# Attention scores by head instead of by pair of heads: products of 64 rows and 72 columns in place of 128 rows and 144 columns, in an attention and mixture-of-experts kernel on one Trainium2 core

## The chip, the cores and the metric

The kernel runs on one core of a Trainium2 chip. The metric is the time of one execution on the device, in microseconds (us). Matrix products run on TensorE (PE in the profile; its loads of the stationary operand are listed apart, as PEld). VectorE is DVE, ScalarE is ACT, GpSimd is POOL, and SP is the engine that issues most of the DMAs.

## The reference

```python
B, H, S, D = 8, 8, 576, 64          # attention
Sp = S // 8                          # 72: keys and values are averaged over 8 rows
k_p = k.reshape(B, H, Sp, 8, D).mean(axis=3)
v_p = v.reshape(B, H, Sp, 8, D).mean(axis=3)
scores = matmul(q, k_p^T) / sqrt(D)  # per head: 576 x 72, over 64 elements
attn = softmax(scores)
x = (attn @ v_p) as 4608 tokens x 512
# mixture of experts: the token's best of 4 groups, then the best of that group's 4 experts
h = relu(x[mask] @ w1[g, e]); ye = h @ w2[g, e]      # 512 -> 1024 -> 512
out[mask] = gate * ye
```

All data is float32.

## The kernel before

The work goes batch by batch (8 batches of 576 tokens). For each batch the attention part pools keys and values, computes scores and their softmax and multiplies by the pooled values; then the batch's most frequent expert is applied to all its tokens (`up`, line 532, and `down`, lines 553 and 563). Tokens of other experts are taken by a loop at the end of the program.

A batch's 576 query rows are five chunks: four of 128 rows and one of 64 (`CH`). For each chunk, `sc` computes the scores of all eight heads. The heads stand in four pairs g. The transposed queries `qT` have a pair's two heads one above the other: 64 partitions of the first head, 64 of the second. The transposed pooled keys `kT` are 128 partitions by 144 columns a pair, with the first head's 72 columns filled in the upper 64 partitions, the second head's 72 columns in the lower 64, and zeros in the two other quarters. So one product a pair, over all 128 partitions, gives both heads' scores side by side. The chunk's query rows are the stationary operand (`lhsT`), `kT` is streamed past it (`rhs`). Each float32 product of this kind appears in the profile as two loads and two MATMULs, so that a chunk's four products are eight of each.

The scores stand in one PSUM tile of two banks (`ss`, two pairs to a bank). From there VectorE takes the maxima (`mx`, line 298) and subtracts them (`sb`, line 304), ScalarE takes the exponential (line 305), VectorE sums (`su_`), GpSimd or VectorE divides (`nm`), and TensorE transposes the probabilities (`px_`, line 331; `pm`, line 343) for the product with the values (`av`, line 358).

The order of the work is written by hand in four lists: START and FIRST for the beginning and batch 0, STEADY for batches 1 to 6, LAST for batch 7. While a batch's expert runs, the next batch's attention is done between its pieces: `m.up:0:0`, then `n.sc:1 n.mx:1 n.sb:1`, then `m.up:0:1`, and so on. TensorE, SP and VectorE follow these lists in program order; ScalarE and GpSimd follow them in START, and GpSimd's and ScalarE's order in the rest is set by the framework's scheduler. `warm` (line 824) are products of a matrix of ones, which fill TensorE's waits at the start.

Of the kernel before, what the change touches and what calls it, by code (L numbers as in the profile page):

```python
# [8 lines left out]
F32 = mybir.dt.float32  # L9
# [4 lines left out]
ALU = mybir.AluOpType  # L14
# [4 lines left out]
SP = 72  # L19
NG = H // 2  # L20
# [65 lines left out]
def attn_moe(ctx: ExitStack, tc: tile.TileContext, q, k, v, wg, we, w1, w2, out):  # L86
    nc = tc.nc
    tt, ts, stt = nc.vector.tensor_tensor, nc.vector.tensor_scalar, nc.vector.scalar_tensor_tensor
# [53 lines left out]
    sm = ctx.enter_context(tc.tile_pool(name="sm", bufs=2))  # L142
# [16 lines left out]
    class Att:  # L159
# [127 lines left out]
        def sc(s, c):  # L287
            n = CH[c][1]
            ps = s.ss[c] = ps_s.tile([128, 2, 512], F32, name="sc")
            for g in range(NG):  # L290
                nc.tensor.matmul(ps[0:n, g // 2, 144 * (g % 2):144 * (g % 2) + 144], lhsT=s.qT[c][:, g, 0:n], rhs=s.kT[:, g, :],  # L291
                                 start=(g % 2 == 0), stop=(g % 2 == 1))

        def mx(s, c):
            n = CH[c][1]
            scv = s.ss[c][0:n, :, 0:288].rearrange("p u (x s) -> p u x s", s=SP)
            mx = s.m[c] = sm.tile([128, 2, 4], F32, name="mx")
            red(out=mx[0:n], in_=scv, axis=AX.X, op=ALU.max)  # L298

        def sb(s, c):  # L300
            n = CH[c][1]
            scv, mx = s.ss[c][0:n, :, 0:288].rearrange("p u (x s) -> p u x s", s=SP), s.m[c]
            p = s.p[c] = sm.tile([128, 2, 4, SP], F32, name="p")
            tt(out=p[0:n], in0=scv, in1=mx[0:n].unsqueeze(3).broadcast_to([n, 2, 4, SP]), op=ALU.subtract)  # L304
            nc.scalar.activation(out=p[0:n], in_=p[0:n], func=AF.Exp)  # L305

        def su_(s, c):
# [568 lines left out]
```

## Time and profile before

| | |
|---|---|
| median of 3 runs | 615.87 us (615.83 to 618.83) |
| the profiled execution | 614.83 us |
| its span, first to last instruction | 612.7 us |
| TensorE (PE) busy | 589.0 us, 96% of the span |
| loads of its stationary operand (PEld) busy | 525.6 us, 86% |
| VectorE, ScalarE, GpSimd busy | 404.8, 281.8, 253.8 us |
| MATMULs of `sc` (line 291) | 320, of 3841 |
| mean granted TensorE clock | 0.988 of full speed |

The profile is of one execution. Around its span lie 2.1 us of the execution's time. Matmuls overlap in time, each starting before the one ahead has ended, so that a group's pace (start to start) is shorter than the duration of one; pieces of the chain of waits, which count each moment once, are read as paces. In a shape such as 128\*64 128x144 the first pair is the stationary operand's partitions and columns, the second the streamed operand's.

### The profile page before, as it was taken

To read this page: it belongs to the slowest core of one execution; us is meant where nothing else is said; L and a number is where in the kernel's file an instruction comes from. 1 tells how busy PE (TensorE), PEld (TensorE's weight loads), DVE (VectorE), ACT (ScalarE), POOL (GpSimd) and SP (SyncE) were. 2 spreads that over 40 slices of the span, in tenths; PEclk is the share of its full clock that TensorE was granted. 3 is DMA by queue.
4 is the path that set the end of the run, shared out by engine and by line. 5 is a ranking of instruction groups with operands and counts; after the bars stand their busy time and mean duration, and the time that the engine had idled before them with its cause. 6 is when DMAs were issued, how large, how long until landed. Compare 5 with 4: busy or idle time off the path is not lost.

```text
span 612.7 us, 10857 instructions
## 1 busy us (share of the span) xinstructions
PE 589.0 (96%) x3841; PEld 525.6 (86%) x3841; DVE 404.8 (66%) x1000; ACT 281.8 (46%) x585; POOL 253.8 (41%) x255
## 2 busy tenths in 40 slices
PE   6969999999999999999999999999999999999996
PEld 5858887789988999789988998789978998899874
DVE  4886998879774696548774696549673783347231
ACT  3544635366444653555344653455434643243121
POOL 3034546056423663275424663275424662253100
PEclk8998999999999999999999999999999999999999
DMA  6476415255517542454517552484517200541911
GB/s 186 101 243 113 157 36 113 77 200 200 112 52 242 171 83 75 138 186 124 110 49 242 173 88 68 148 347 115 112 39 245 92 1 2 177 176 26 381 68 40
DMA packets 118761, 81.30 MB, mean 133 GB/s; under 512 B 76327, under 2 KB 95271, under 8 KB 118321
## 3 DMA queue, kind: packets, MB, share of 16 engines
q1 hardware_dynamic: 112656, 70.83, 39.4%
q10 hardware_dynamic: 6016, 9.70, 4.4%
q8 instruction: 32, 0.52, 0.4%
q14 instruction: 25, 0.20, 0.1%
q0 software_dynamic: 32, 0.04, 0.0%
HBM read 75.01 MB, written 28.38 MB: 169 GB/s over the span
## 4 chain that ended last, share of the span: by engine, by line
PE 78%; DVE 13%; DMA 3%; ACT 2%; issue 2%; SPq 1%; POOL 0%; DVEq 0%; POOLq 0%
PE mm L532 28%; PE mm L553 26%; PE sc L291 5%; PE tp L358 5%; PE mm L563 5%; DVE kp L208 3%; PE tp L343 2%; DMA kv<-in_v_dram 2%; DMA sw<-in_moe_w_dram 1%; DVE ht L539 1%; PE tp L331 1%; ACT kb L226 1%; PE tp L371 1%; DVE px L320 1%; DVE xt L363 1%
## 5 line engine op out<-in xcount | busy, mean ns | idle before, releaser
L532 PE MATMUL mm<-xt,w 128*128 128x256 f32 (+1 forms) x1536 | 224.5, 301 | 3.8 <-DVE ht L539 1.6
L532 PEld LDWEIGHTS mm<-xt,w 128*128 128x128 f32 x1536 | 208.7, 190 | 7.1 <-issue 1.7
L553 PE MATMUL mm<-w,ht 128*128 128x512 f32 x768 | 187.7, 396 | 0.0
L518 POOL TENSOR_TENSOR w<-sw,w 128x1024 fp32r<-128x1024 f32 x54 | 131.7, 2456 | 95.2 <-ACT w L517 90.9
L553 PEld LDWEIGHTS mm<-w,ht 128*128 128x128 f32 x768 | 140.8, 188 | 29.3 <-issue 0.8
L534 ACT ACTIVATE ht<-mm 128x256 fp32r<-128x256 f32 (+1 forms) x128 | 52.2, 408 | 112.2 <-PE mm L532 110.8
L539 DVE SCALAR_TENSOR_TENSOR ht<-mm,ht 128x256 fp32r<-128x256 f32 (+1 forms) x192 | 60.5, 344 | 35.0 <-ACT ht L534 34.9
L517 ACT CAST w<-sw 128x1024 fp32r<-128x1024 f32 x64 | 65.5, 1048 | 23.2 <-DMA sw<-in_moe_w_dram 13.4
L320 POOL TENSOR_TENSOR px<-p,su 128x96 f32<-128x96 f32 (+1 forms) x72 | 24.5, 360 | 96.3 <-DVE su L312 53.2
L298 DVE TENSOR_REDUCE mx<-sc 128x8 f32<-128x576 f32 (+1 forms) x40 | 29.9, 748 | 36.5 <-PE sc L291 36.5
L291 PE MATMUL sc<-kT,qT 128*128 128x144 f32 (+1 forms) x320 | 47.4, 292 | 0.0
L291 PEld LDWEIGHTS sc<-kT,qT 128*128 128x128 f32 (+1 forms) x320 | 42.6, 184 | 2.3 <-issue 1.6
L324 POOL TENSOR_TENSOR p<-p,su 128x576 f32<-128x576 f32 (+1 forms) x36 | 41.4, 1149 | 2.8
L558 ACT ACTIVATE y<-mm,gm 128x512 f32<-128x512 f32 x32 | 21.9, 684 | 36.8 <-PE mm L553 36.7
L305 ACT ACTIVATE p<-p 128x576 f32<-128x576 f32 (+1 forms) x40 | 27.3, 683 | 21.8 <-DVE p L304 21.7
L310 DVE TENSOR_REDUCE su<-p 128x8 f32<-128x576 f32 (+1 forms) x40 | 29.9, 746 | 8.9 <-ACT p L305 7.9
L569 DVE TENSOR_TENSOR y<-mm,y 64x512 f32<-64x512 f32 x8 | 5.5, 682 | 44.7 <-ACT y L568 44.7
L363 DVE TENSOR_TENSOR xt<-tp,xt 128x320 fp32r<-128x320 f32 (+2 forms) x68 | 29.3, 437 | 7.9 <-ACT xt L359 6.2
L359 ACT CAST xt<-tp 128x320 fp32r<-128x320 f32 (+2 forms) x68 | 26.1, 384 | 17.1 <-PE tp L358 15.1
L208 DVE TENSOR_REDUCE kp<-kv 128x128 f32<-128x1024 f32 x16 | 31.0, 1971 | 2.7 <-DMA kv<-in_k_dram 2.7
L304 DVE TENSOR_TENSOR p<-sc,mx 128x576 f32<-128x576 f32 (+1 forms) x40 | 30.2, 754 | 3.3
L230 POOL TENSOR_TENSOR kv<-kv 128x512 f32<-128x512 f32 x13 | 16.8, 1292 | 32.8 <-DMA kv<-in_v_dram 32.3
(206 smaller groups left out, 739.0 us busy)
## 6 DMA issues: line engine op xcount, KB each, us to landing
sw<-in_moe_w_dram SPq DMA_DIRECT2D x72, 512.0 KB
xscr<-xt SPq DMA_DIRECT2D x8, 2304.0 KB
kv<-in_k_dram SPq DMA_DIRECT2D x16, 512.0 KB
kv<-in_v_dram SPq DMA_DIRECT2D x16, 512.0 KB
out_dram<-y ACTq DMA_DIRECT2D x32, 256.0 KB
q<-in_q_dram SPq DMA_DIRECT2D x112, 72.0 KB
kv<-in_moe_w_dram SPq DMA_DIRECT2D x6, 512.0 KB
ph<-xscr SPq DMA_DIRECT2D x2, 1152.0 KB
```

What stands on the lines that cost most here:

```text
L208: red(out=s.kp[:, 2 * u:2 * u + 2, :], in_=s.k[u].rearrange("p g (j d) -> p g d j", j=8), axis=AX.X, op=ALU.add)
L291: nc.tensor.matmul(ps[0:n, g // 2, 144 * (g % 2):144 * (g % 2) + 144], lhsT=s.qT[c][:, g, 0:n], rhs=s.kT[:, g, :], start=(g % 2 == 0), sto ...
L324: eng.tensor_tensor(out=p[0:n], in0=p[0:n], in1=su[0:n].unsqueeze(3).broadcast_to([n, 2, 4, SP]), op=ALU.mult)
L358: nc.tensor.matmul(ps[:, 0:n], lhsT=flat(l[:, g]), rhs=r, start=(i == 0), stop=(i == len(ops) - 1))
L363: tt(out=s.xt[:, 1, g, sl], in0=s.ta[g][:, 0:n], in1=s.xt[:, 0, g, sl].bitcast(F32), op=ALU.subtract)
L517: nc.scalar.copy(out=wh, in_=raw)
L518: (nc.vector if eng == "v" else nc.gpsimd).tensor_tensor(out=wl, in0=raw, in1=wh.bitcast(F32), op=ALU.subtract)
L532: nc.tensor.matmul(ps[:, 0:n], lhsT=l[:, kc, fs], rhs=xt[:, r, kc, sl], start=(kc == 0 and i == 0), stop=(kc == 3 and i == 2))
L534: nc.scalar.activation(out=ht[:, sl], in_=ps[:, 0:n], func=AF.Relu)
L539: stt(out=ht[:, at:at + hi - lo], in0=ps[:, lo - o:hi - o], scalar=0.0, in1=ht[:, lo:hi].bitcast(F32), op0=ALU.max, op1=ALU.subtract)
L553: nc.tensor.matmul(ps, lhsT=s.ht[f][:, 640 * l + o:640 * l + o + 128], rhs=s.w[2, f // 2][r][:, f % 2, :], start=(i == 0), stop=(i == 23))
L563: nc.tensor.matmul(ps, lhsT=s.ht[f][:, 512:640], rhs=s.w[2, f // 2][r][:, f % 2, :], start=(i == 0), stop=(i == 15))
```

## The change

`sc` computes each head by itself. For a pair g and a head x of it, the product takes the 64 partitions of that head in `qT` and `kT` and the 72 columns that are filled, so that the quarters of zeros are no longer streamed. A chunk has eight products in place of four, each of half the partitions and half the columns. The heads x = 0 go to the first bank of the PSUM tile and the heads x = 1 to the second. `mx` and `sb` read the tile by another access pattern (pair, then bank, then the 72 columns), and `sb` writes the probabilities in the order in which they stood before. The number of elements is the same in each.

```diff
         def sc(s, c):
             n = CH[c][1]
             ps = s.ss[c] = ps_s.tile([128, 2, 512], F32, name="sc")
             for g in range(NG):
-                nc.tensor.matmul(ps[0:n, g // 2, 144 * (g % 2):144 * (g % 2) + 144], lhsT=s.qT[c][:, g, 0:n], rhs=s.kT[:, g, :],
-                                 start=(g % 2 == 0), stop=(g % 2 == 1))
+                for x in range(2):
+                    r = slice(64 * x, 64 * x + 64)
+                    nc.tensor.matmul(ps[0:n, x, SP * g:SP * g + SP], lhsT=s.qT[c][r, g, 0:n], rhs=s.kT[r, g, SP * x:SP * x + SP],
+                                     start=(g == 0), stop=(g == NG - 1))
 
         def mx(s, c):
             n = CH[c][1]
-            scv = s.ss[c][0:n, :, 0:288].rearrange("p u (x s) -> p u x s", s=SP)
-            mx = s.m[c] = sm.tile([128, 2, 4], F32, name="mx")
+            scv = s.ss[c][0:n, :, 0:288].rearrange("p x (g s) -> p g x s", s=SP)
+            mx = s.m[c] = sm.tile([128, NG, 2], F32, name="mx")
             red(out=mx[0:n], in_=scv, axis=AX.X, op=ALU.max)
 
         def sb(s, c):
             n = CH[c][1]
-            scv, mx = s.ss[c][0:n, :, 0:288].rearrange("p u (x s) -> p u x s", s=SP), s.m[c]
+            scv, mx = s.ss[c][0:n, :, 0:288].rearrange("p x (g s) -> p g x s", s=SP), s.m[c]
             p = s.p[c] = sm.tile([128, 2, 4, SP], F32, name="p")
-            tt(out=p[0:n], in0=scv, in1=mx[0:n].unsqueeze(3).broadcast_to([n, 2, 4, SP]), op=ALU.subtract)
+            pv = p[0:n].rearrange("p u (y x) s -> p (u y) x s", x=2)
+            tt(out=pv, in0=scv, in1=mx[0:n].unsqueeze(3).broadcast_to([n, NG, 2, SP]), op=ALU.subtract)
             nc.scalar.activation(out=p[0:n], in_=p[0:n], func=AF.Exp)
```

On TensorE, in a batch's steady part, the chunks' scores (`sc`) stand between `up` products (`mm<-xt,w`). Before (the program counts a float32 product once here, and prints the output's size):

```order
L532 MATMUL mm<-xt,w 128x256 x12
L291 MATMUL sc<-kT,qT 128x144 x4
L532 MATMUL mm<-xt,w 128x320 x12
L532 MATMUL mm<-xt,w 128x256 x12
L331 MATMUL tp<-ident,px 96x128 x2
L343 MATMUL tp<-ident,p 128x128 x4
L532 MATMUL mm<-xt,w 128x320 x12
L291 MATMUL sc<-kT,qT 64x144 x4
```

The same places on TensorE now, where every line number from `sc` on has grown by three or four:

```order
L536 MATMUL mm<-xt,w 128x256 x12
L294 MATMUL sc<-kT,qT 128x72 x8
L536 MATMUL mm<-xt,w 128x320 x12
L536 MATMUL mm<-xt,w 128x256 x12
L335 MATMUL tp<-ident,px 96x128 x2
L347 MATMUL tp<-ident,p 128x128 x4
L536 MATMUL mm<-xt,w 128x320 x12
L294 MATMUL sc<-kT,qT 64x72 x8
```

Nothing else moved on TensorE: four products became eight at each of the 40 places (32 chunks of 128 rows, 8 of 64), and all around them stands as it stood. SP's order is the same too, and VectorE's but for buffer numbers.

On ScalarE the scheduler moved a few instructions by one place. Near the start of a steady batch, before (`ht<-mm` is the `up` piece's relu, `p<-p` the exponential of a chunk's scores, `y<-y,gm` the last rows of the batch before):

```order
L570 ACTIVATE y<-y,gm 64x512
L571 DMA out_dram<-y 64x512
L534 ACTIVATE ht<-mm 128x320
L305 ACTIVATE p<-p 128x576
L534 ACTIVATE ht<-mm 128x256
L332 CAST pr<-tp 96x2x128
```

And now, at the same place on ScalarE:

```order
L574 ACTIVATE y<-y,gm 64x512
L575 DMA out_dram<-y 64x512
L309 ACTIVATE p<-p 128x576
L538 ACTIVATE ht<-mm 128x320
L538 ACTIVATE ht<-mm 128x256
L336 CAST pr<-tp 96x2x128
```

The exponential now stands ahead of one relu that it followed. This recurs once in each steady batch; in FIRST and in the first steady batch there are three more such exchanges on ScalarE, and one on GpSimd.

## Rows read from the trace of the kernel before

**Rows 1.** The page: busy time by engine, TensorE's granted clock in 40 slices.

```profile
PE 589.0 (96%) x3841; PEld 525.6 (86%) x3841; DVE 404.8 (66%) x1000; ACT 281.8 (46%) x585; POOL 253.8 (41%) x255
...
PEclk8998999999999999999999999999999999999999
```

**Rows 2.** Windows by stage: length, busy time of each engine (instructions), clock, DMA.

```profile
0.00:62.00 62.00, 49.55 (x352) 44.21 (x353) 43.38 (x82) 28.32 (x63) 19.02 (x42) 0.89 0.60 159
62.00:125.50 63.50, 60.23 (x380) 52.21 (x379) 56.08 (x141) 29.99 (x72) 24.65 (x30) 1.00 0.38 107
...
194.08:262.66 68.58, 68.51 (x437) 61.68 (x437) 46.21 (x111) 33.88 (x70) 32.00 (x31) 1.00 0.45 133
```

**Rows 3.** The chain of waits, in order of time, in one steady batch.

```profile
208.64 1.75 PE mm L532 x12
210.39 0.98 PE sc L291 x8
211.37 3.18 PE mm L532 x24
...
221.47 1.76 PE mm L532 x12
223.23 1.12 PE sc L291 x8
224.35 3.38 PE mm L532 x24
```

**Rows 4.** The chain of waits in START and FIRST, batch 0.

```profile
22.69 0.98 PE sc L291 x8
...
30.08 8.05 DMA sw<-in_moe_w_dram
...
50.98 1.58 PE sc L291 x8
```

**Rows 5.** Timeline around a chunk of 128 rows, TensorE and its loads.

```profile
134.95 1.05 PEld L291 LDWEIGHTS sc<-kT,qT 128*128 128x128 f32 x8
135.07 1.15 PE L291 MATMUL sc<-kT,qT 128*128 128x144 f32 x8
```

**Rows 6.** Timeline around a chunk of 64 rows, in brackets the idle time before.

```profile
154.59 0.93 PEld L291 LDWEIGHTS sc<-kT,qT 128*64 128x64 f32 x8 [0.19 <-issue]
154.59 1.19 PE L291 MATMUL sc<-kT,qT 128*64 128x144 f32 x8
155.72 0.19 PEld L532 LDWEIGHTS mm<-xt,w 128*128 128x128 f32 x1 [0.20 <-issue]
```

**Rows 7.** Timeline: loads behind which little is streamed, 128 and 64 partitions.

```profile
23.39 0.98 PEld L454 LDWEIGHTS tp<-wr,ht 128*128 128x128 f32 x8
...
575.25 0.29 PEld L701 LDWEIGHTS tp<-kT,q 64*128 64x128 f32 x2
```

**Rows 8.** Groups of loads by form: busy us, mean ns of one.

```profile
L291 PEld LDWEIGHTS sc<-kT,qT 128*128 128x128 f32 x256 | 34.8, 194 | 0.7 <-issue 0.2
L291 PEld LDWEIGHTS sc<-kT,qT 128*64 128x64 f32 x64 | 7.8, 143 | 1.6 <-issue 1.4 <-PE tp L343 0.2
L701 PEld LDWEIGHTS tp<-kT,q 64*128 64x128 f32 x2 | 0.3, 184 | 0.0
L448 PEld LDWEIGHTS tp<-ht,rp 32*64 32x64 f32 x8 | 0.7, 130 | 0.7 <-issue 0.7
```

**Rows 9.** Timeline in START: one part of the array, then two column halves by turns.

```profile
19.22 0.19 PEld L448 LDWEIGHTS tp<-ht,rp 32*64 32x64 f32 x2 [0.17 <-issue]
19.57 0.20 PEld L446 LDWEIGHTS tp<-ht,vp 128*64 128x64 f32 x4 [0.17 <-issue]
...
19.22 0.43 PE L448 MATMUL tp<-ht,rp 32*64 32x128 f32 x2
19.58 0.44 PE L446 MATMUL tp<-ht,vp 128*64 128x128 f32 x4
```

**Rows 10.** Timeline: transposes of a 64-row chunk, 64 partitions, between full-height products.

```profile
162.94 0.17 PEld L331 LDWEIGHTS tp<-ident,px 64*96 64x96 f32 x2 [0.19 <-issue]
163.05 0.33 PEld L343 LDWEIGHTS tp<-ident,p 64*128 64x128 f32 x4
...
163.10 0.41 PE L343 MATMUL tp<-ident,p 64*128 64x64 f32 x4
```

**Rows 11.** The page: groups of VectorE that read the scores.

```profile
L298 DVE TENSOR_REDUCE mx<-sc 128x8 f32<-128x576 f32 (+1 forms) x40 | 29.9, 748 | 36.5 <-PE sc L291 36.5
...
L304 DVE TENSOR_TENSOR p<-sc,mx 128x576 f32<-128x576 f32 (+1 forms) x40 | 30.2, 754 | 3.3
```

**Rows 12.** Timeline of ScalarE in a steady batch, around a chunk's exponential.

```profile
206.58 0.44 ACT L534 ACTIVATE ht<-mm 128x320 fp32r<-128x320 f32 x1 [1.60 <-PE mm L532]
206.91 0.68 ACT L305 ACTIVATE p<-p 128x576 f32<-128x576 f32 x1
208.02 0.38 ACT L534 ACTIVATE ht<-mm 128x256 fp32r<-128x256 f32 x1 [0.43 <-PE mm L532]
```

## The prediction

> **What bounds the kernel now.** I read the page first. TensorE is busy for 96% of the span, and its granted clock is at full speed (the level of 2.4 GHz) in all but the first few slices [rows 1]. Busy shares are averages, so the windows by stage come next: in a steady batch TensorE is busy for 68.51 of 68.58 us, while the next busiest engine, VectorE, has 46.21 [rows 2]. What TensorE takes longer or shorter there goes into the time whole. Only the first two stages have idle time on it: 12.5 us in the first 62 us, 3.3 us in the next 63.5 [rows 2]. The chain of waits confirms the place: in a steady batch it runs along TensorE from piece to piece, and each chunk's scores stand in it with 0.98 us at 128 rows and 1.12 us at 64 [rows 3]. Of batch 0's five chunks only the second and the last stand in the chain; behind the second comes a weight transfer of 8.05 us [rows 4].
>
> So I count 7 batches with four chunks of 128 rows on the path, and one of batch 0's: 29 of 32. Of the 64-row chunks all 8 count.
>
> **What a chunk's scores cost now.** Eight MATMULs of 144 columns in 0.98 us are 0.122 us each. The eight loads run beside them and start with the same steps (1.05 us against 1.15 for the eight) [rows 5]: streaming sets the pace, loads are hidden.
>
> How fast could loads alone go? Where only 20 columns are streamed behind a load, eight loads take 0.98 us; one lasts 0.19, so the step is (0.98 - 0.19)/7 = 0.112 us for 128 columns of stationary operand. With 64 partitions and the same 128 columns, two loads take 0.29, one 0.184: a step of 0.29 - 0.184 = 0.11 us [rows 7, 8]. Half the partitions save nothing. Columns do: 64 of them last 0.143 us and 32 partitions with 64 columns 0.130, against 0.194 for 128 columns [rows 8], and two of 0.130 end within 0.19 [rows 9], a step of 0.06.
>
> **The change, part by part.** *Streaming.* 72 columns should take half of 144: 0.061 us a MATMUL.
>
> *Loads.* The products double and their loads do not shrink at 128 rows: 16 loads of 128 columns in place of 8. The two heads of a pair use different halves of the array. If the halves work side by side, each has 8 loads one after another, at 0.112 us a step, and the streaming (0.061) hides under them. If one waits for the other, a step for both is 0.224. No row shows two halves that lie one above the other. The nearest shows two halves side by side: four loads and four MATMULs in two column halves take 0.20 and 0.44 us, where two loads and two MATMULs in a single part take 0.19 and 0.43 [rows 9]. I take 0.112, with 0.061 and 0.224 as the bounds.
>
> The Trainium skill, TensorEngine Tiling (Array Packing), Key Properties, says that tiles are independent and can load and multiply in parallel. By that rule the step is 0.112; the trace agrees for column halves, and no run here shows row halves yet.
>
> *Passing to a smaller part of the array and back.* This is the part of which the diff says nothing. Wherever the trace goes from full-size products to a smaller part, the load waits 0.17 to 0.20 us and is not fetched ahead: at the 64-row chunk going in and coming out [rows 6], at 64-partition transposes [rows 10], in START [rows 9]. A chunk of 128 rows shows no such gap now [rows 5]. Its price comes from the chain: a 64-row chunk with the `up` products around it takes 1.76 + 1.12 + 3.38 = 6.26 us, a 128-row chunk with the same number around it 1.75 + 0.98 + 3.18 = 5.91 [rows 3]. The eight MATMULs are equally wide, so passing in and out costs 0.35 us. In it lies the first load, bare, of 64 columns; at 128 columns that is 0.112 - 0.06 = 0.05 more. So 0.40 us for each 128-row chunk, newly paid, since its products are now of half height; the 64-row chunks pay their 0.35 already.
>
> *A chunk of 128 rows* then takes 0.40 + 7 steps of 0.112 + 0.061 for the last streaming = 1.245 us against 0.98: 0.265 more. 29 of them: +7.7 us.
>
> *A chunk of 64 rows* has loads of 64 columns, 0.06 a step, that just hide under 0.061 of streaming: 8 x 0.061 = 0.49 against 0.98, and the same passing: 0.49 less. 8 of them: -3.9 us.
>
> *VectorE.* The maxima and the subtraction read the same 576 elements in runs of 72, in another order: 748 and 754 ns [rows 11]. I take no change. If each took half as long again, that is 0.75 us a chunk, 3.8 us a batch, on an engine with 22 us to spare there [rows 2]; what it would hide behind is the next `up` products on TensorE, 3.18 us after each chunk [rows 3].
>
> *ScalarE.* The exponential that now stands ahead of a relu takes 0.68 us [rows 12]. That relu is late by 0.5 to 0.7 us, and what waits behind it, the `upd` subtraction, frees one of three PSUM tiles of `up`. TensorE comes back to that tile two `up` pieces later, some 3 us (24 products take 3.18 [rows 3]). I put it at nothing; without that cover it would be 0.6 us a batch, 4 us in all.
>
> **The sum.** 7.7 - 3.9 = +3.8 us. All 32 chunks on the path would make +4.6, batch 1's hidden in the idle time of its stage +3.2. The error of the passing price (0.05 a chunk) is 1.5 us either way, that of the load step (0.106 to 0.12) -1.2 to +1.6. The profiled execution took 614.83 us (span 612.7 and 2.1 around it), so it becomes 618.6. The median of the runs, 615.87, lies 1.0 above the profiled execution, and I forecast the median: 619.6 us, with its own range of 616.5 to 623. A change under 0.5% (3.1 us) is what a measurement of this kernel can hardly tell from none, and the forecast lies just outside.
>
> **The rivals.** *The halves take turns at loading.* A step for both halves is then 0.224 us: 0.40 + 7 x 0.224 + 0.061 = 2.03, or 1.05 more a chunk, +30.4 us for 29. The 64-row chunks would gain only 0.98 - 8 x 0.12 = 0.02. About 645 us. For it speaks only that no row shows row halves; against it, the column halves [rows 9].
>
> *A load waits for its own half's MATMUL to end.* A step is 0.112 + 0.061 = 0.173 and a 128-row chunk takes 0.69 more: +20 us, with little gained at 64 rows, about 636 us. Against it: full-height loads run beside MATMULs of the same rows today [rows 5], and the four 64-partition loads from 163.05 to 163.38 run over the four transposes from 163.10 to 163.51 [rows 10].
>
> The Trainium skill, TensorE: Matmul & The Clock Gate, The mechanism, has that rule: a load overlaps with MATMULs in flight only if their row groups differ. By it this rival would hold; rows 5 and 10 show overlap on the same rows, so I give it little.
>
> *Faster.* This would need one thing: that in half-height products loads cost no more than the streaming. At a step of 0.061 a 128-row chunk takes 0.40 + 0.43 + 0.06 = 0.89, and all gain: 29 x -0.09 - 3.9 = -6.5, about 609 us. The two kinds of chunk balance at a step of 0.093 (29 x (7 x 0.093 - 0.519) = 3.8). The 0.11 of the 64-partition load [rows 7] speaks against it, though it is a single pair.
>
> The Trainium skill, TensorEngine Tiling, Theoretical Speedup, promises up to twice the speed for a dimension of 64 or less. Taken as half the time of each chunk it would give more than this rival; rows 7 have loads that do not halve.
>
> *Nothing to measure.* A step of 0.10, or a passing price nearer 0.35, leaves +1 to +2 us: 617 to 618.
>
> **Chances.** The forecast (side-by-side halves, loads set the pace) 0.72; turns 0.12; loads that wait 0.03; faster 0.05; nothing to measure 0.08. Within the forecast I give 0.20 to the part under 3.1 us. So slower 0.52 + 0.15 = 0.67, same 0.20 + 0.08 = 0.28, faster 0.05. The range takes in the forecast and "nothing to measure" and leaves out the rest, 0.20: 615 to 624.
>
> **What the profile after would show.** 128-row chunks: 16 MATMULs of 64\*128 by 72 in pairs that start together, pairs 0.11 us apart; in the chain 0.8 to 0.9 us for the scores themselves, 0.2 us of waiting for nothing named at each load that goes in or out, and `up` products behind them at 3.38 in place of 3.18. 64-row chunks: pairs 0.06 apart. A steady batch: 68.58 + 4 x 0.265 - 0.49 = 69.15 us, with VectorE and ScalarE as busy as now. I am wrong if pairs don't start together (a batch then takes some 4 us more), if they come faster than 0.09, or if the gaps on going in and out are missing: then 29 x 0.40 = 11.6 us fall away, and the time is some 608.

## The result and the profile after

| | before | after |
|---|---|---|
| median of 20 runs each | 615.85 us (614.39 to 620.35) | 624.55 us (618.62 to 626.76) |
| ratio of the times | | 1.0106, interval 1.0081 to 1.0131 |
| the profiled execution | 614.83 us | 624.49 us |
| its span | 612.7 us | 622.3 us |
| its mean granted clock | 0.988 | 0.976 |

The change makes the kernel slower. The times of after stand on two levels: 13 of the 20 took 624.0 to 626.8 us at a mean granted clock of 0.972 to 0.979, the other seven 618.6 to 621.9 at 0.982 to 0.992. Before has two levels as well, 13 runs at 614.4 to 616.4 us and seven at 618.4 to 620.4. These 20 have no clock on record; of 40 more runs of before, timed beside the experiments, six took 618.6 to 619.4 us, at 0.982 to 0.987, and none of the 40 had a clock under 0.982. The ratio lies below that of the medians (1.014), because the middle time of before falls on its lower level and that of after on its upper. A ratio goes by the runs within 1.5% of the fastest of their kernel, which leaves out one run here, 624.45 us of sc0_half.

Applied to 615.85 the ratio gives 622.4 us, inside the range of 615 to 624; the median of 624.55 lies 0.55 above it. The lowest times differ by 618.62 - 614.39 = 4.2 us, close to the forecast of +3.8. What the forecast did not have is the upper level of after, with its lower clock.

The page after: TensorE's busy time and clock, the groups of `sc`, and those of VectorE that read the scores (lines 291, 298 and 304 before, now 294, 301 and 308).

```profile
PE 599.2 (96%) x4161; PEld 527.6 (85%) x4161; DVE 402.6 (65%) x1000; ACT 281.1 (45%) x585; POOL 253.2 (41%) x255
...
PEclk8597999999999999999999999999999999999999
...
L308 DVE TENSOR_TENSOR p<-sc,mx 128x576 f32<-128x576 f32 (+1 forms) x40 | 30.2, 754 | 3.3
...
L301 DVE TENSOR_REDUCE mx<-sc 128x8 f32<-128x576 f32 (+1 forms) x40 | 29.9, 748 | 36.3 <-PE sc L294 35.9
```

Against [rows 1] TensorE is busy for 10.2 us more, and the second of the clock's 40 digits is 5 where it was 9. VectorE's two groups are where they were, 748 and 754 ns [rows 11].

The chain of waits of after in the steady batch of [rows 3], and the start of the next batch:

```profile
200.63 1.05 PE sc L294 x16
201.68 3.85 PE mm L557 x16
...
215.68 1.75 PE mm L536 x12
217.43 1.04 PE sc L294 x16
218.48 3.38 PE mm L536 x24
...
229.03 1.76 PE mm L536 x12
230.79 0.65 PE sc L294 x16
231.43 3.38 PE mm L536 x24
...
269.71 1.05 PE sc L294 x16
```

A chunk of 128 rows with the `up` products around it now takes 1.75 + 1.04 + 3.38 = 6.17 us, where [rows 3] have 5.91: 0.26 more. A chunk of 64 rows takes 1.76 + 0.65 + 3.38 = 5.79 in place of 6.26: 0.47 less. From one batch's first scores to the next one's, 200.63 to 269.71, are 69.08 us; before, the same two marks lie 68.58 apart [rows 2].

Timeline of after around the 128-row chunk, TensorE:

```profile
217.36 1.11 PE L294 MATMUL sc<-kT,qT 64*128 64x72 f32 x16
```

The same of its loads:

```profile
217.36 0.97 PEld L294 LDWEIGHTS sc<-kT,qT 64*128 64x128 f32 x16 [0.19 <-issue]
```

Sixteen loads end within 0.97 us: the eight of a half would need 7 x 0.112 + 0.19 = 0.97 by themselves, so the other half's eight lie beside them. Ahead of the first load stands the idle 0.19 us that [rows 6] show around a 64-row chunk and [rows 5] don't show.

The windows by stage of after, against [rows 2]:

```profile
0.00:62.00 62.00, 52.46 (x368) 45.70 (x369) 39.77 (x76) 26.00 (x57) 14.56 (x38) 0.78 0.55 146
...
194.08:262.66 68.58, 68.51 (x474) 60.88 (x474) 45.54 (x110) 33.29 (x70) 32.22 (x30) 1.00 0.45 130
```

The steady stage has the same idle time on TensorE as before (0.07 us) and full speed. The first stage had a clock of 0.89 and has 0.78. So the 9.6 us between the two spans come from two places. Where batch 2's first scores begin (125.35 us before, 131.45 after), 6.1 us are already lost. The six batches whose scores follow make 3.0 at +0.50 each; 0.5 I did not place.

The start, in windows of TensorE before (busy time, granted clock, DMA share and GB/s). These rows are not among those of the prediction:

```profile
16.00:18.00 2.00, 2.00 (x12) 0.57 0.42 20
18.00:20.00 2.00, 1.70 (x16) 1.00 0.91 190
20.00:32.00 12.00, 11.91 (x104) 1.00 0.46 129
```

And after:

```profile
14.00:16.00 2.00, 2.00 (x11) 0.50 0.26 52
16.00:18.00 2.00, 2.00 (x17) 0.50 0.40 22
18.00:20.00 2.00, 2.00 (x14) 0.50 0.89 181
20.00:32.00 12.00, 12.00 (x64) 0.50 0.17 40
32.00:34.00 2.00, 2.00 (x18) 0.88 0.36 89
```

A granted clock of 0.50 is the level of 1.2 GHz, 1.00 that of 2.4. Before, TensorE comes to full speed between 16 and 18 us, while it works on batch 0's first scores; after, only between 32 and 34. In the 12 us from 20 to 32 it is busy throughout in both, and gets through 104 MATMULs before and 64 after.

What stands on TensorE where the clock did not rise, timeline of after:

```profile
16.45 1.99 PE L294 MATMUL sc<-kT,qT 64*128 64x72 f32 x16
18.37 1.11 PE L278 MATMUL tp<-ident,q 128*128 128x128 f32 x4
```

The same transposes in the timeline of before:

```profile
17.95 0.60 PE L278 MATMUL tp<-ident,q 128*128 128x128 f32 x4
```

Before, these four ran at full speed, in 0.60 us where there are now 1.11. The chain of waits of after, at batch 0's first two chunks, at the routing behind them (`wr`, line 458), at the weights that it chooses and at batch 0's last chunk:

```profile
16.52 1.92 PE sc L294 x16
...
26.02 1.92 PE sc L294 x16
27.94 1.84 PE tp L458 x8
...
35.37 8.20 DMA sw<-in_moe_w_dram
...
56.37 0.70 PE sc L294 x16
```

The second chunk's scores begin at 26.02 in place of 22.69 us [rows 4], 3.3 later, and take 1.92 in place of 0.98. The routing's products are then 4.3 late and take 1.84 us, where the chain of before has 0.81 (from 23.68 us). Together that is the +5.3 with which the transfer starts, at 35.37 in place of 30.08 us; the last chunk's scores follow at 56.37 in place of 50.98 [rows 4], +5.4. The first chunk now stands in the chain too; before, VectorE's work behind a transfer of values stood there.

### The profile page after: what moved, and what is told of

Read it like the earlier page. It is cut to its first block, busy times and chain, and to the rows that moved or that the text cites. A ratio compares the mean times of both kernels' runs of the same rounds, so it can differ in the third digit from the quotient of the medians.

```text
span 622.3 us, 11497 instructions
## 1 busy us (share of the span) xinstructions
PE 599.2 (96%) x4161; PEld 527.6 (85%) x4161; DVE 402.6 (65%) x1000; ACT 281.1 (45%) x585; POOL 253.2 (41%) x255
## 4 chain that ended last, share of the span: by engine, by line
PE 77%; DVE 13%; DMA 3%; ACT 2%; SPq 2%; issue 2%; POOL 1%; DVEq 0%; POOLq 0%
PE mm L536 28%; PE mm L557 25%; PE sc L294 5%; PE tp L362 5%; PE mm L567 5%; DVE kp L208 3%; PE tp L347 2%; DMA q<-in_q_dram 1%; DMA sw<-in_moe_w_dram 1%; DVE ht L543 1%; PE tp L335 1%; ACT kb L226 1%; PE tp L375 1%; DVE px L324 1%; DVE xt L367 1%
## 5 line engine op out<-in xcount | busy, mean ns | idle before, releaser
L294 PEld LDWEIGHTS sc<-kT,qT 64*128 64x128 f32 (+1 forms) x640 | 37.3, 183 | 7.8 <-issue 4.2
L294 PE MATMUL sc<-kT,qT 64*128 64x72 f32 (+1 forms) x640 | 43.2, 276 | 0.0
```

Of the source, the lines that this page charges most:

```text
L294: nc.tensor.matmul(ps[0:n, x, SP * g:SP * g + SP], lhsT=s.qT[c][r, g, 0:n], rhs=s.kT[r, g, SP * x:SP * x + SP], start=(g == 0), stop=(g == ...
```

## The experiments

The first four kernels behind after let some chunks go head by head and the rest by pair; pass_only is the kernel before with one product added, and the last three change one thing in the products of all chunks. The steady theory is that of the prediction (16 loads side by side, passing in and out), the clock theory that the half-height products of the start cost some 5 us more through TensorE's clock.

| kernel | head by head are | median us | ratio to before, interval |
|---|---|---|---|
| after | all 40 chunks | 624.55 | 1.0106 (1.0081 to 1.0131) |
| start_full | all but batch 0's four of 128 rows | 621.78 | 1.0084 (1.0052 to 1.0116) |
| start_half | batch 0's first three | 620.1 | 1.0064 (1.0038 to 1.009) |
| sc0_half | batch 0's first | 615.3 | 1.0016 (0.9983 to 1.0049) |
| c4_only | the eight of 64 rows | 612.91 | 0.9954 (0.9933 to 0.9976) |
| pass_only | none; one small product behind each of 28 chunks | 626.14 | 1.016 (1.0119 to 1.0201) |
| same_half | all, on one half, without the second heads | 654.04 | one run |
| full72 | all, over 128 partitions | 641.19 | one run |
| x_outer | all, first one half's four products | 642.31 | one run |

The kernel before, timed beside them, stood at medians of 615.24 us (for start_full, start_half, c4_only, same_half) and 615.32 (for the others).

**start_full: the start by pair, the rest head by head.**

```diff
+        def half(s, c):
+            return s.b > 0 or c == 4
...
         def sc(s, c):
             n = CH[c][1]
             ps = s.ss[c] = ps_s.tile([128, 2, 512], F32, name="sc")
+            if not s.half(c):
+                for g in range(NG):
+                    nc.tensor.matmul(ps[0:n, g // 2, 144 * (g % 2):144 * (g % 2) + 144], lhsT=s.qT[c][:, g, 0:n], rhs=s.kT[:, g, :],
+                                     start=(g % 2 == 0), stop=(g % 2 == 1))
+                return
...
```

What is left out lets `mx` and `sb` read either layout.

> Batch 0's first four chunks by pair of heads, as before; all other chunks by head. Theory A (two causes: in the steady batches the passing in and out and the loads, 7 x 0.5 = 3.5 us; at the start the half-height products, under which TensorE's clock stays at half longer): the start is as before, clock 0.89 in the first 62 us, whole run 3 to 4 us above before, 619 to 619.5. Theory B (the longer half clock at the start is chance, not the products' height): it stays as often as with the whole change, median 622 to 624.5.

Measured: 618.91 to 622.87 us in six runs. The start is nearly as before again, in the windows of this kernel; the clock is up between 18 and 20 us:

```profile
16.00:18.00 2.00, 2.00 (x11) 0.50 0.39 21
18.00:20.00 2.00, 2.00 (x17) 0.89 0.88 176
20.00:32.00 12.00, 11.93 (x104) 1.00 0.46 130
```

No run had a mean clock under 0.980, where 13 of 20 had it with the change. Two of the six stand at 0.980, a little under the lowest of before (0.982), and no trace shows their start. So the long stretch at 1.2 GHz hangs on batch 0's 128-row chunks, at least for the most part. But the median is some 2.5 us above what was expected. The profiled execution (622.67) shows 2.1 us of it, in a place of its own: in the first steady batch TensorE waits 2.06 us for VectorE. VectorE there:

```profile
135.53 2.63 DVE L339 TENSOR_TENSOR px<-p,su 128x96 f32<-128x96 f32 x2
138.19 2.84 DVE L343 TENSOR_TENSOR p<-p,su 128x576 f32<-128x576 f32 x1
```

GpSimd in the same stretch:

```profile
132.82 2.40 POOL L537 TENSOR_TENSOR w<-sw,w 128x1024 fp32r<-128x1024 f32 x1 [3.85 <-ACT w L536]
135.66 4.76 POOL L537 TENSOR_TENSOR w<-sw,w 128x1024 fp32r<-128x1024 f32 x2 [0.43 <-ACT w L536]
```

Beside the two products of GpSimd (135.66 to 140.42) VectorE's two lines last 2.63 us (two operations) and 2.84. In the profile before they last 0.43 and 0.76 and start between two such products, at 132.80 and 133.26 us; GpSimd's end at 132.50 and start again at 133.50. ScalarE's cast ahead of GpSimd waits 1.78 us for a weight transfer here. The Trainium skill, GPSIMD Engine Reference, Specifications, says that GpSimd shares its way to SBUF with VectorE and that instructions with two SBUF inputs contend; these two have two, and the rows agree. How often this meeting happens, and whether the change has a part in it, these runs don't settle: c4_only's profiled execution has it too, and some runs of before lie on a level that would fit it (3 of the 23 beside this kernel at 618.8 to 619.4 us, seven of the first 20 at 618.4 to 620.4), though no trace was kept of one.

**start_half: only the start head by head.** The edit is start_full's, with

```diff
-            return s.b > 0 or c == 4
+            return s.b == 0 and c < 3
```

> Only batch 0's first three chunks by head; all others by pair, as before. Theory A: steady batches of 68.58 us as before, the start at half clock for some 20 us in most executions, median 619 to 622. Theory B: as before within 1 us, 615 to 617.

Measured: 10 of 12 runs at 619.75 to 621.57 us (clock 0.972 to 0.984), two at 614.82 and 615.08 (0.991, 0.993). In its profile the first 62 us have a clock of 0.78 and the steady batch is that of before:

```profile
0.00:62.00 62.00, 52.86 (x349) 46.17 (x350) 39.16 (x76) 25.55 (x56) 14.22 (x38) 0.78 0.56 149
194.08:262.66 68.58, 68.51 (x437) 61.67 (x436) 46.22 (x111) 32.96 (x70) 32.28 (x30) 1.00 0.45 129
```

So three chunks of the start alone cost about 5 us, in most executions. Three chunks at the +0.265 of a steady chunk would cost 0.8 at most.

**sc0_half: only the first chunk of all.** Again against start_full:

```diff
-            return s.b > 0 or c == 4
+            return s.b == 0 and c == 0
```

> Only batch 0's first chunk by head; everything else by pair, as before. Theory A1 (that chunk's half-height products, streamed while the clock is at half, alone keep it there; before, the same chunk at full height came just ahead of the rise): most executions as in the run with three such chunks, median 619 to 621. Theory A2 (it takes the later chunks of the start too): as before, 615 to 616.

Measured: seven of 12 at 613.88 to 615.49 us (clock 0.988 to 0.993), five at 619.78 to 624.45 (0.974 to 0.980); none of the 17 runs of before beside it was at 0.980 or under. Neither expectation holds in its pure form: one chunk is enough to keep the clock down, but not each time. Runs at a mean clock of 0.980 or less are 5 of 12 with one such chunk, 9 of 12 with three, 13 of 20 with all; that more chunks do it more often is not shown by so few runs.

**c4_only: only the 64-row chunks.** Against start_full:

```diff
-            return s.b > 0 or c == 4
+            return c == 4
```

> Only the eight chunks of 64 rows by head; all chunks of 128 rows by pair, as before. Theory A (the price of passing in and out is already paid there, loads of 64 columns hide under the streaming; 1.12 to 0.65 us a chunk in the chain): 8 x -0.47 = -3.8 us, 611.5 to 612.5, steady batches 68.1 us. Rival (what the chunk gains, a later wait takes back, since the consumers of the scores set the pace there): 615 to 616.

Measured: 612.91 us, ratio 0.9954 (0.9933 to 0.9976), 2.3 to 2.8 us less than before by median and ratio. The chain in one of its steady batches:

```profile
289.54 0.98 PE sc L295 x8
290.52 3.20 PE mm L551 x24
294.37 1.76 PE mm L551 x12
296.13 0.65 PE sc L301 x16
296.78 3.38 PE mm L551 x24
```

The 128-row chunk keeps 0.98 and 3.20, the 64-row chunk has 0.65. Eight times 0.47 are 3.8 us, of which the time shows 2.3 to 2.8; where the rest goes is open. This version beats both kernels, if narrowly.

**pass_only: the kernel before with the passing alone.** Behind each 128-row chunk from batch 1 on stands one small product of half height and half width (64 rows, 64 columns, two MATMULs), whose result nobody reads.

```diff
+            if s.b > 0 and c < 4:
+                nc.tensor.matmul(ps[0:64, 1, 288:296], lhsT=s.qT[c][0:64, 0, 0:64], rhs=s.kT[0:64, 0, 0:8], start=True, stop=True)
```

> All products as before; behind the four of each 128-row chunk, from batch 1 on, one small product more, of 64 rows by 64 columns with 8 columns streamed, into columns that nobody reads. Theory A (each passing to a smaller part of the array and back costs some 0.35 us, first loads included): two small loads more (0.06) and the passing, some 0.4 us a chunk, a steady batch 70.1 us, the run 10 to 12 us above before, 625 to 628. Rival (passing costs little; what a half-height chunk pays more lies in its loads): a steady batch of 68.9 us, 617 to 619.

Measured: 626.14 us, 10.8 above before, 0.386 for each of 28 chunks (by the ratio 9.8, or 0.35). The chain:

```profile
283.76 0.98 PE sc L291 x8
284.74 0.21 PE sc L294 x2
284.95 3.38 PE mm L534 x24
```

0.21 us stand before the `up` products and 0.20 in them (3.38 against 3.18), 0.41 in this place. Going to a smaller part of the array and back costs what the prediction took from the 64-row chunk, with next to no work done there.

**same_half: both heads on one half of the array.** The second head's scores are left out by it: the lower half's rows are never read. So the chain of a steady batch is compared and not the whole time.

```diff
-                    r = slice(64 * x, 64 * x + 64)
+                    r = slice(0, 64)
```

> Both heads' products on the upper 64 partitions (the second head's scores are then not computed: the products take the first head's rows and the quarter of zeros), same number and shape of products, two banks as in the change. Theory A (the two halves of the array load and stream side by side, and a half takes its loads one after another at 0.112 us): a 128-row chunk takes 0.40 + 15 x 0.112 + 0.06 = 2.1 us in place of 1.25, a steady batch some 72.5 us, the run 645 to 655. Rival (the pairs only look simultaneous, and the banks or the number of products set the pace): as the change, a steady batch of 69.1 us.

Measured: 654.04 us. The chain at a 128-row chunk:

```profile
301.45 1.93 PE sc L301 x16
303.39 3.38 PE mm L551 x24
```

And its loads in the timeline:

```profile
301.38 1.86 PEld L301 LDWEIGHTS sc<-kT,qT 64*128 64x128 f32 x16 [0.19 <-issue]
```

1.93 us in place of 1.05: with one half the 16 loads stand in a row, (1.86 - 0.19) / 15 = 0.111 apart. So with two halves they are side by side. And a step of 0.111 has no room for 0.061 of streaming besides the load: loads run beside the MATMULs of their own half. The Trainium skill, TensorE: Matmul & The Clock Gate, The mechanism, has it otherwise in one sentence (only row groups that differ overlap), while another there lets a load also go ahead into a background weight buffer; these rows decide against the first.

**full72: head by head, but over all 128 partitions.** The streamed columns are 72, half of whose rows are the zeros of `kT`.

```diff
-                    nc.tensor.matmul(ps[0:n, x, SP * g:SP * g + SP], lhsT=s.qT[c][r, g, 0:n], rhs=s.kT[r, g, SP * x:SP * x + SP],
+                    nc.tensor.matmul(ps[0:n, x, SP * g:SP * g + SP], lhsT=s.qT[c][:, g, 0:n], rhs=s.kT[:, g, SP * x:SP * x + SP],
```

> Head by head with 72 columns and two banks as in the change, but over all 128 partitions (the other head's quarter is zeros), so one array part for all. Theory A (loads set the pace at 0.112 us once streaming is 0.061, and nothing is paid for passing): a 128-row chunk takes 16 x 0.112 = 1.8 us in the chain, the products behind it stay at 3.20, a steady batch 71.8 us, the run 638 to 642. Rival (loads of so narrow products hide as before, 0.061 a step): 0.98 us a chunk, 615 to 617.

Measured: 641.19 us. The chain:

```profile
293.85 1.74 PE sc L300 x16
295.59 3.24 PE mm L550 x24
```

Sixteen full-height loads in 1.74 us are 0.109 each, with 72 columns streamed behind each: loads set the pace at full height too. The `up` products take 3.24 and not 3.38, so passing is gone; behind its 64-row chunks, whose loads have 64 columns, they still take 3.38. Passing is bound to the part of the array that a product takes, not to the number of products. The start of this kernel bears on the clock:

```profile
16.00:18.00 2.00, 2.00 (x17) 0.82 0.38 23
18.00:20.00 2.00, 1.90 (x19) 1.00 0.83 161
```

With as many products as in the change, and as wide, but at full height, the clock rises as early as before; in the traces of same_half and x_outer, at half height, it is at 0.50 until past 32 us. That points to the height. But each is one execution, and in some of the change's own the clock is not held down either.

**x_outer: the change with its two loops exchanged.** One half's four products stand ahead of the other's.

```diff
-            for g in range(NG):
-                for x in range(2):
+            for x in range(2):
+                for g in range(NG):
```

> The change with its two loops swapped: all four products of the first head's half, then all four of the second's. Theory A (TensorE starts the other half's loads far ahead of the order in which they are written): 1.05 us a chunk as in the change, a steady batch of 69.1 us. Rival B (it looks ahead only some instructions, so halves run side by side only where they alternate): up to 0.40 + 15 x 0.112 + 0.06 = 2.1 us with the passing, a steady batch up to 72.5 us, the run 640 to 655.

Measured: 642.31 us. The chain:

```profile
296.27 1.55 PE sc L301 x16
297.81 3.38 PE mm L551 x24
```

1.55 us lie between the 1.05 of halves side by side and the 1.93 of one half. In the trace of one such chunk the first half's loads start at 206.960 us and the second half's at 207.467, 0.51 later, just as the fifth of the first half's eight MATMULs began (207.463). From there the two run side by side until the first half is through. So the other half's loads are fetched ahead, but only from so far: the overlap hangs on the order in which the program writes the two heads.

## Why the prediction was right in direction and short in size

The steady part of the forecast came true term by term. That the 622.4 us of the ratio lie in its range is in part luck: the range was not drawn for what the start did, and in most executions the start cost more than the whole forecast of +3.8.

**Loads set the pace at 128 rows: right.** The step of 0.112 taken from a row of 20 streamed columns and a single pair of 64-partition loads [rows 7] shows in after (16 loads in 0.97 us), in same_half (0.111) and in full72 (0.109).

**The halves work side by side: right.** same_half separates it: 1.93 against 1.05 us. The rival of turns (645) would have given after what same_half has. x_outer adds a condition that the prediction did not know, a close alternation in the program; the change has it.

**A load that waits for its own half's MATMUL: falls** with the steps of same_half.

**Passing in and out, 0.40 a chunk: right.** pass_only, with smaller products, has 0.386 as a mean of 28 (0.35 by the ratio) and 0.41 in the chain; in after itself it is 0.19 us ahead of the first load and 0.20 in the `up` products behind (3.38 against 3.18). It is the term that turns the change into a loss: without it a 128-row chunk would be 0.14 shorter than before by the prediction's own sum (1.245 - 0.40 = 0.845 against 0.98).

**The 64-row chunks, -0.49: measured -0.47,** and c4_only shows the gain by itself.

**A steady batch, 69.15 forecast, 69.08 measured.** Of the 0.07, some 0.06 lies in the 128-row chunks, of which some cost 0.24 and not 0.265: ahead of `down`, scores and `down` take 1.05 + 3.85 = 4.90 us, where the marks of before, 194.08 and 198.74 in the chain, lie 4.66 apart. The 64-row chunk goes the other way by 0.02; the rest is not placed.

**VectorE and ScalarE at nothing: right in the steady batches.** The groups of `mx` and `sb` kept their durations, and TensorE's idle time there did not grow.

**The start, taken at one chunk of +0.265 on the path: this step failed.** The prediction read that only the second and the last of batch 0's chunks stand in the chain [rows 4], and priced all of the start with durations from steady batches, at 2.4 GHz. Rows 1 and 2 had the low clock of the first slices in sight, but no sentence asked what ends it. In after the first chunk stands in the chain as well, and from 14 to 32 us TensorE runs at 1.2 GHz. In the profiled execution the second chunk's scores come 3.3 us later, the transfer behind them 5.3 and batch 0's last chunk 5.4; start_half gives the same 5 us without the rest of the change, and start_full takes most of the low clock away. Another 1.0 us of the 6.1 at batch 2 is a wait of TensorE for GpSimd in FIRST, which stood behind a transfer of `kv` that the late start had pushed back on SP's queue; that was read from the trace of after alone, not tried.

That batch 0's 128-row chunks, in the form that the change gives them, keep the clock down is shown by start_half and start_full. That it is their height, and not their number or width, full72 points to with one execution. Why one chunk does so in some executions and not in others is not shown, and by what the clock rises at 32 us isn't either: TensorE was busy throughout from 14 us on.

What stays open besides is the 2.5 us by which start_full lies above its sum, and the upper level in the times of before.

## What to carry to other kernels

Here products on half of the array's height paid where their loads had few columns and the passing was paid already: at 64 columns a chunk of scores fell from 1.12 to 0.65 us, at 128 the doubled loads and 0.4 us of passing in and out took more than the halved streaming gave. Before counting streamed columns, look for the idle time around the nearest smaller products in the trace; write the halves in close alternation, and let a change go only where its sum is negative (c4_only). Price the first stage with its own granted clock, and ask of each change there whether it touches the work during which the clock rises.

## What was not expected of the hardware

With full-height scores TensorE came to 2.4 GHz at 16 to 20 us in the profiles; with 16 half-height MATMULs in their place it stayed at 1.2 GHz until 32 to 34 us in the profiles of after and start_half, though busy throughout; one such chunk is enough in some executions (sc0_half). A half's loads wait 0.51 us when four products of the other half are written ahead of them (x_outer). Loads run beside the MATMULs of their own half, 0.111 us apart (same_half). And VectorE's lines of 0.43 and 0.76 us lasted 2.63 and 2.84 beside GpSimd's products (start_full).
